# The first batch's first 512 feed-forward columns as single float32 matmuls, and the second batch's scores computed with the states in the rows

## The chip, the core and the metric

The kernel runs on one core of one Trainium2 chip. The metric is the device time of one execution in microseconds (us); three runs of the kernel before gave 684.73, 686.70 and 690.73, so the median is 686.7 us. TensorE (PE) multiplies matrices, VectorE (DVE) and ScalarE (ACT) work on elements, and SyncE (SP) issues the DMA transfers.

## The reference

The inputs are `x` (8 batches, 8 heads, 512 tokens, 64 wide), `state` (8, 8, 32 states, 64) and the weights `w_in` (512 x 2048) and `w_out` (2048 x 512). The weights come as float64 numbers, which the kernel itself turns into float32; the rest is float32.

```python
scores = scale * np.matmul(x, state.transpose(0, 1, 3, 2))     # tokens look at states
a = softmax(scores);  xread = np.matmul(a, state)
scores2 = scale * np.matmul(state, x.transpose(0, 1, 3, 2))    # states look at tokens
a2 = softmax(scores2); sread = np.matmul(a2, x)
attn = np.concatenate([xread, sread], axis=2)                  # 512 + 32 rows per batch
x = attn.transpose(0, 2, 1, 3).reshape(B * S, H * D)           # 4352 tokens of 512
h = x @ w_in;  g = h * np.clip(h + 3.0, 0.0, 6.0) / 6.0;  out = g @ w_out
```

## The kernel before, in words

**Two feed-forward products in float32r.** The feed-forward layer takes nearly all the time. TensorE computes it in float32r, a short form of float32, and makes up for the lost digits by splitting every operand into a high and a low part: `product` (L642) issues three matmuls, high x high, high x low and low x high, for each pair. The high part is a ScalarE cast and the low part a VectorE subtraction (`split`, L242). So every operand, the token weights `aT`, the projected weights `wp`, the hidden values `g` and `w_out`, costs one ScalarE and one VectorE instruction per tile before TensorE may use it.

**Steps.** The first product folds the attention read into `w_in`: `wprime` (L424) computes state x `w_in` once per batch and 512-column chunk, and `first` (L653) multiplies it with the token softmax `aT`: 2 groups of heads x 3 matmuls of 128x512 for each of 128 columns of the hidden layer (a step). ScalarE and VectorE then apply the activation into `g`, and `second` (L693) adds `g` times `w_out` to four accumulators: 4 products of 3 matmuls. There are 16 steps for a batch; the first two batches are interleaved by segments: batch 0 steps 0 to 3 (chunk 0), batch 1 steps 0 to 7, the rest of batch 0, the rest of batch 1, then the others in turn.

**Two ways to the token softmax.** `tokens_by_rows` (L507, batches 0 and 1 before) computes scores with the tokens in the rows: 2 x 8 float32 matmuls of 128x64 (L527), the softmax (`softmax_parts`, L479), then transposes on TensorE (L544) and the split. `scores_by_columns` (L551) with `tokens_by_columns` (L559, the other batches) computes 8 small matmuls of 64x32 weights and 512 columns each (L419), and VectorE transposes blocks of 32x32 before and after the softmax. The state softmax (`states`, L573) needs the second form in any case; batches 0 and 1 compute it later, at their eighth to twelfth step.

**Weights.** Each weight tile arrives as 64-bit words. ScalarE (L294, L298) and VectorE (L302, L306, L313) turn the words into float32; `w_out` is then split into halves (L335, L337). Tiles go through `raw` buffers or through `early0` to `early3`, which share space with later tiles.

**What sets the order.** The code hands every operation to `Plan` with a cost, a rank and its dependencies; `Plan.order` (L54) plays them through in a model of the four queues and writes the order in which each engine gets its instructions. Each engine then works its own list strictly in that order, so a waiting instruction holds all behind it. Until the first feed-forward matmul, the gaps that the plan foresees on TensorE are filled with transposes of the identity (L901). All loads are issued by SP, in the planned order.

Of the kernel before, what the change touches and what calls it, by code (L numbers as in the profile page):

```python
# [20 lines left out]
class Plan:  # L21
# [32 lines left out]
    def order(self):  # L54
# [93 lines left out]
def tile_state_attention_then_hardswish_ffn(  # L148
# [51 lines left out]
    w_in_sb = cpool.tile([P, NQ, DFF], F32, name="w_in_sb")  # L200
# [13 lines left out]
            "g_hi": 3, "g_lo": 3, **{f"early{k}": 1 for k in range(4)}, **BANKS,  # L214
# [34 lines left out]

    HOMES = [(c, half) for c in range(NCH - 2, NCH) for half in ("hi", "lo")]  # L250
    w_out_sb = {}

    def w_out_key(k, half):
        home = (k // FPC, half)
        return (f"early{HOMES.index(home)}", "home", k) if home in HOMES else ("w_out", k, half)
# [9 lines left out]
    def weight(kind, k, n, place, rank, load_rank):  # L265
# [44 lines left out]
        def sign():  # L310
            low, high, _, _ = words()
            d = w_in_sb[:, :, ks].bitcast(U32) if kind == "in" else low
# [11 lines left out]
        if kind == "in":  # L324
            V(wide, rank, sign, [hi, lo], [("w_in", f) for f in range(k, k + n)])
            return
        V(wide, rank, sign, [hi], [lo])
        low = lambda: words()[0].bitcast(F32)
        at_home = {h: [w_out_key(f, h) for f in range(k, k + n)] for h in ("hi", "lo")}

        gone = [
            m for slot, users in plan.users.items() for m in users
            if slot[1] != "home" and slot[0] in (at_home["hi"][0][0], at_home["lo"][0][0])
        ]
        S_((0.6, 1.05)[n - 1], rank, lambda: nc.scalar.copy(w_out_of("hi", k, n), low()),  # L335
           [lo], at_home["hi"], gone)
        V(wide, rank, lambda: nc.vector.tensor_tensor(  # L337
            w_out_of("lo", k, n), low(),
            w_out_of("hi", k, n).bitcast(F32),
            op=ALU.subtract), [lo, *at_home["hi"]], at_home["lo"])  # L340
# [6 lines left out]
    def load_state(b, rank, after=()):  # L347
# [6 lines left out]
        plan.add("Q", 0.9, rank, load, (), [key], after, 64.0)  # L354
# [69 lines left out]
    def wprime(b, c, f0, f1, rank, banks=None, after=()):  # L424
# [5 lines left out]
        def wp(half):  # L430
# [5 lines left out]
            lambda q: w_in_sb[:, q, c * CH + f0 * P : c * CH + f1 * P]),  # L436
            [("stT", b)] + [("w_in", c * FPC + f) for f in range(f0, f1)], bs, after)
        for u in range(NG):
# [5 lines left out]
    def tmp(key):  # L444

        return get(key, lambda: att.tile([P, S], F32, name="tmp", bufs=10))

    def take_in(b, rank, after=(), banks=None):
# [10 lines left out]
        for q in range(NQ):  # L459
            xT = ("tmp", ("xT", b, q))  # L460
            if b >= TURNED:
                key = ("raw", ("x", b, q // 2))
                V(0.7, rank, lambda q=q, key=key, xT=xT: nc.vector.transpose(
                    tmp(xT), made[key][:, q % 2]),
                    [(*key, q % 2, u, k) for u in range(2) for k in range(D // NS)], [xT], after)
                continue
# [10 lines left out]
            S_(0.6, rank, lambda ps=ps, xT=xT: nc.scalar.copy(tmp(xT), bank(ps)), [ps], [xT])  # L477
# [29 lines left out]
    def tokens_by_rows(b, rank, after, banks=None):  # L507
# [14 lines left out]
        def scores(k):  # L522
            out = bank(ps[k]).rearrange("p (j u q n) -> p j q u n", j=J // 2, u=NG, n=NS)
            for j in range(J // 2):
                for q in range(NQ):
                    js = slice((k * J // 2 + j) * P, (k * J // 2 + j + 1) * P)
                    nc.tensor.matmul(  # L527
                        out[:, j, q], tmp(("tmp", ("xT", b, q)))[:, js], apart[:, q],
                        start=True, stop=True,
                    )  # L530
        for k in range(2):
            scores_at[b] = T(2.0, rank(1), lambda k=k: scores(k),
                             [("apart", u) for u in range(NG)]
                             + [("tmp", ("xT", b, q)) for q in range(NQ)], [ps[k]], after(1))
        for k in range(2):
# [4 lines left out]
            def turn(back=back, bt_key=bt_key):  # L540
                for g in range(NG):
# [3 lines left out]
            T(0.47, rank(4), turn, [bt_key], [back], after(4))  # L545
            split(min(rank(4), 0.0), lambda k=k: hi_lo["hi"]()[:, :, half(k)],
                  lambda k=k: hi_lo["lo"]()[:, :, half(k)],
                  lambda back=back: bank(back).rearrange("p (g t) -> p g t", g=NG),
                  [back], [("aT", b, k, "hi"), ("aT", b, k, "lo")])

    def scores_by_columns(b, rank, after=()):  # L551

        ps = [("ps_s", ("C", b, u)) for u in range(NG)]
        T(1.2, rank, lambda: all_heads(
            b, [bank(k) for k in ps], lambda q: tmp(("tmp", ("xT", b, q)))),
          [("stT", b)] + [("tmp", ("xT", b, q)) for q in range(NQ)], ps, after)
# [41 lines left out]
    def state_read(b, rank, after):  # L598
# [17 lines left out]
        for u in range(NG):  # L616
# [22 lines left out]
            [scores_at[1]])  # L639
# [13 lines left out]
    def first(n):  # L653
        b, i, _, _ = steps[n]
        ps = ("ps_h", n)
        if b < B:
# [6 lines left out]
            reads += [("wp", (b, k), f0, u, h) for u in wide for h in ("hi", "lo")]  # L663
        else:
# [6 lines left out]
        def run():  # L671
            ah, al = (made["aT", b][h]() for h in ("hi", "lo"))
# [5 lines left out]
        first_of[n] = T(1.37 if b < B else 1.45, n, run, reads, [ps], first_after.get(n, ()))  # L678


        g = lambda: get(("g", n), lambda: gp.tile([P, S], F32, name="g"))[:, :width]
# [4 lines left out]
            g(), bank(ps)[:, :width], AF.Relu, bias=three), [ps], [("g", n)])  # L686
        V(cost, n, lambda: nc.vector.scalar_tensor_tensor(  # L687
            g(), g(), 6.0, bank(ps)[:, :width], op0=ALU.min, op1=ALU.mult), [ps], [("g", n)])
        split(n, half["hi"], half["lo"], g, [("g", n)], [("g_hi", n), ("g_lo", n)], cost)
# [3 lines left out]
    def second(n):  # L693
# [3 lines left out]
        for j in range(nt):  # L697
# [7 lines left out]
            T(0.685, n + LAG + 0.5, run,  # L705
              [("g_hi", n), ("g_lo", n), w_out_key(i, "hi"), w_out_key(i, "lo")], [acc])
# [34 lines left out]
    def w_in_split(c, rank, after):  # L741

        cs = slice(c * CH // 2, (c + 1) * CH // 2)
        wp = {h: (lambda h=h: get((f"wp_{h}", (B, c)), lambda: gp.tile(
            [P, NQ, CH // 2], F32R, name=f"wp_{h}"))) for h in ("hi", "lo")}
        S_(1.2, rank, lambda: nc.scalar.copy(wp["hi"](), w_in_sb[:, :, cs]), [],
           [("wp", (B, c), "hi")], after)
        V(1.25, rank, lambda: nc.vector.tensor_tensor(
            wp["lo"](), w_in_sb[:, :, cs], wp["hi"]().bitcast(F32), op=ALU.subtract),
# [17 lines left out]
    for seg, (b, c0, c1) in enumerate(segments):  # L767
# [109 lines left out]
    for n in range(len(steps)):  # L877
# [54 lines left out]
```

## Time and profile before

| | |
|---|---|
| median of three runs | 686.7 us |
| the profiled execution | 687.1 us, of which the span of its records is 685.3 us |
| PE busy | 668.7 us (98%) |
| DVE busy | 418.1 us (61%) |
| ACT busy | 318.4 us (46%) |
| first feed-forward matmul starts | 29.41 us |

The span is the time from the first to the last record; the execution's own time is 1.8 us more. PE counts as busy also where matmuls overlap in its pipeline, so a row's length is more than its share of the stream: the distance between the starts of two matmuls tells what one costs.

### The profile page before, as it was taken

Reading aid. Unit: us, or ns where it says so; the run is one execution under the profiler, and the core shown is the slowest. Engines: PE = TensorE matmul, PEld = TensorE weight load, DVE = VectorE, ACT = ScalarE, POOL = GpSimd, SP = SyncE. Lnnn points to the kernel's source line nnn. Section 1 sums busy time; section 2 is a strip of 40 time slices with the busy share of each in tenths; the row PEclk is TensorE's granted clock in tenths of the full one; section 3 lists DMA queues with packets and bytes.
Section 4 is the critical chain, followed back from the end, with each engine's and each line's share of the span. In section 5 each row is a group of like instructions: output and inputs, shape, how many; then the busy total and the mean of one; then the engine's idle time right before and its main releaser. Section 6 shows DMA issues by size and latency. Waiting matters only on the chain.

```text
span 685.3 us, 10084 instructions
## 1 busy us (share of the span) xinstructions
PE 668.7 (98%) x4095; PEld 517.2 (75%) x4095; DVE 418.1 (61%) x729; ACT 318.4 (46%) x533; POOL 1.0 (0%) x7
## 2 busy tenths in 40 slices
PE   7798999999999999999999999999999999999997
PEld 6676677777777777787777777777777777778996
DVE  3889888859865835844486337934584444334552
ACT  4886667554523533533354333533443344333442
POOL 0000000000000000000000000000000000000000
PEclk9999999999999999999999999999999999999999
DMA  8731144343244020511040302330010001000101
GB/s 258 271 124 62 62 134 119 122 93 89 39 123 67 1 62 0 128 36 27 1 111 16 62 1 71 58 62 0 1 62 1 1 0 63 1 0 1 63 1 31
DMA packets 94126, 41.54 MB, mean 61 GB/s; under 512 B 82432, under 2 KB 84480, under 8 KB 93952
## 3 DMA queue, kind: packets, MB, share of 16 engines
q1 hardware_dynamic: 94080, 40.90, 22.6%
q8 instruction: 32, 0.52, 0.3%
q14 instruction: 14, 0.11, 0.1%
HBM read 31.98 MB, written 8.91 MB: 60 GB/s over the span
## 4 chain that ended last, share of the span: by engine, by line
PE 93%; SPq 2%; ACT 1%; DVE 1%; DMA 1%; issue 0%
PE acc L648 56%; PE ps_h L648 28%; PE ps_s L419 6%; PE ps_s L621 1%; PE ps_s L606 1%; DMA early<-in_moe_w_out_dram 1%; SPq L374 1%; SPq L353 1%; PE ps_s L527 1%; SPq L289 0%; ACT early L294 0%; ACT early L298 0%; ACT aT_hi L244 0%; DVE g L687 0%; DVE early L306 0%
## 5 line engine op out<-in xcount | busy, mean ns | idle before, releaser
L648 PE MATMUL acc<-w_out_hi,g_hi 128*128 128x512 f32 x544 | 220.7, 406 | 0.0
L648 PE MATMUL acc<-w_out_hi,g_lo 128*128 128x512 f32 x544 | 212.9, 391 | 0.0
L648 PE MATMUL acc<-w_out_lo,g_hi 128*128 128x512 f32 x544 | 212.3, 390 | 0.0
L685 ACT ACTIVATE g<-ps_h,three 128x512 f32<-128x512 f32 (+1 forms) x144 | 95.5, 663 | 209.3 <-PE ps_h L648 206.7
L687 DVE SCALAR_TENSOR_TENSOR g<-g,ps_h 128x512 f32<-128x512 f32 (+1 forms) x144 | 94.0, 653 | 141.3 <-ACT g L685 141.0
L648 PEld LDWEIGHTS acc<-w_out_hi,g_hi 128*128 128x128 f32 x544 | 102.4, 188 | 51.5 <-ACT g L685 21.4
L245 DVE TENSOR_TENSOR g_lo<-g,g_hi 128x512 fp32r<-128x512 f32 (+1 forms) x144 | 94.4, 657 | 58.3 <-ACT g_hi L244 57.3
L244 ACT CAST g_hi<-g 128x512 fp32r<-128x512 f32 (+1 forms) x144 | 85.7, 596 | 81.0 <-DVE g L687 80.9
L648 PE MATMUL ps_h<-aT_hi,wp_hi 128*128 128x512 f32 (+1 forms) x320 | 118.9, 372 | 2.6 <-DVE g L687 1.9
L648 PEld LDWEIGHTS acc<-w_out_hi,g_lo 128*128 128x128 f32 x544 | 102.2, 188 | 22.7
L648 PE MATMUL ps_h<-aT_lo,wp_hi 128*128 128x512 f32 (+1 forms) x320 | 118.2, 369 | 0.2 <-DVE aT_lo L245 0.2
L648 PE MATMUL ps_h<-aT_hi,wp_lo 128*128 128x512 f32 (+1 forms) x320 | 118.3, 370 | 0.0
L648 PEld LDWEIGHTS acc<-w_out_lo,g_hi 128*128 128x128 f32 x544 | 102.6, 189 | 18.7
L648 PEld LDWEIGHTS ps_h<-aT_hi,wp_hi 128*128 128x128 f32 x320 | 60.4, 189 | 15.2 <-DVE g L687 2.8
L648 PEld LDWEIGHTS ps_h<-aT_lo,wp_hi 128*128 128x128 f32 x320 | 60.4, 189 | 11.0 <-DVE aT_lo L245 0.5
L648 PEld LDWEIGHTS ps_h<-aT_hi,wp_lo 128*128 128x128 f32 x320 | 60.4, 189 | 10.1
L245 DVE TENSOR_TENSOR wp_lo<-ps_s,wp_hi 128x512 fp32r<-128x512 f32 (+1 forms) x70 | 41.8, 630 | 3.2 <-ACT wp_hi L244 3.2
L244 ACT CAST wp_hi<-ps_s 128x512 fp32r<-128x512 f32 (+1 forms) x70 | 35.2, 542 | 4.7 <-PE ps_s L419 4.6
L419 PE MATMUL ps_s<-w_in_sb,stT 64*32 64x512 f32 (+1 forms) x560 | 35.1, 558 | 1.7 <-DVE w_in_sb L313 1.7
L294 ACT ACTIVATE early<-early,eighth 128x1024 uint32<-128x1024 uint32 (+1 forms) x16 | 18.1, 1129 | 2.6 <-DMA early<-in_moe_w_out_dram 2.0
L609 ACT COPY tmp<-ps_s 128x512 f32<-128x512 f32 x16 | 9.3, 587 | 21.3 <-PE ps_s L606 21.3
L493 ACT ACTIVATE tmp<-tmp 128x512 f32<-128x512 f32 x16 | 10.1, 631 | 17.1 <-DVE tmp L491 16.6
(91 smaller groups left out, 409.1 us busy)
## 6 DMA issues: line engine op xcount, KB each, us to landing
out_dram<-ot SPq DMA_DIRECT2D x8, 1024.0 KB, 5.5
early<-in_moe_w_in_dram SPq DMA_DIRECT2D x7, 1024.0 KB, 5.4
xb<-in_x_dram SPq DMA_DIRECT2D x24, 256.0 KB, 4.7
raw<-in_x_dram SPq DMA_DIRECT2D x96, 64.0 KB, 2.3
early<-in_moe_w_out_dram SPq DMA_DIRECT2D x5, 1024.0 KB, 7.4
raw<-in_moe_w_out_dram SPq DMA_DIRECT2D x4, 512.0 KB
ot<-in_x_dram SPq DMA_DIRECT2D x2, 512.0 KB, 3.7
early<-in_moe_w_in_dram SPq DMA_DIRECT2D x2, 512.0 KB
```

Of the source, the lines that this page charges most:

```text
L244: S_(cost, rank, lambda: nc.scalar.copy(hi(), src()), reads, [writes[0]])
L245: V(cost, rank, lambda: nc.vector.tensor_tensor(lo(), src(), hi().bitcast(F32), op=ALU.subtract), [*reads, writes[0]], [writes[1]])
L294: nc.scalar.activation(low, low, AF.Identity, scale=0.92 * 2.0**-29, bias=eighth)
L353: nc.sync.dma_start(raw[:, u, :], st_v[b, :, :, u, :])
L374: nc.sync.dma_start(x_tile(b)[:, :, j, :], x_v[b, j])
L419: nc.tensor.matmul(out[u][cols, :], made["stT", b][rows, cols], moving(q)[rows], start=True, stop=True,)
L493: S_(0.62, rank(2), lambda: nc.scalar.activation(bt(), bt(), AF.Exp, scale=SCALE), [], [bt_key])
L527: nc.tensor.matmul(out[:, j, q], tmp(("tmp", ("xT", b, q)))[:, js], apart[:, q], start=True, stop=True,)
L609: S_(0.6, URGENT, lambda pe=pe, t_key=t_key: nc.scalar.copy(tmp(t_key), bank(pe)), [pe], [t_key])
L648: nc.tensor.matmul(ps, l, r, start=start and k == 0, stop=stop and k == n - 1)
L685: S_(cost + 0.05, n, lambda: nc.scalar.activation(g(), bank(ps)[:, :width], AF.Relu, bias=three), [ps], [("g", n)])
L687: V(cost, n, lambda: nc.vector.scalar_tensor_tensor(g(), g(), 6.0, bank(ps)[:, :width], op0=ALU.min, op1=ALU.mult), [ps], [("g", n)])
```

## The change

Four things change. (1) `plain(b, c)` is true for batch 0, chunk 0, the first four steps. For these, `wprime` copies the projected weights once as float32 (no halves), `first` issues 2 float32 matmuls instead of 6 float32r ones, the hidden values are not split, and `second` issues one float32 matmul per product instead of three. Its right operand is the decoded `w_out` as it lies in the 64-bit words, that is, every second 32-bit word. The halves of this part of `w_out` and of batch 0's token softmax are still needed for later steps and are made later (`late_halves`, `halves_of_first`). (2) Batch 1's token softmax is computed with `scores_by_columns` and `tokens_by_columns`; the same scores are computed a second time, later, for the state softmax, as batch 0 does. (3) `w_in`, one tile before, is four tiles, and the turned `x` of batches 0 and 1 and batch 0's softmax lie in tiles not yet in use. The first `w_out` pieces are loaded one by one through `raw`. (4) In `Plan.order`, an operation on TensorE that follows another on TensorE is no longer counted as waiting for its latency.

```diff
@@ Plan.order
-                ready[h] = max(ready[h], done)
+                own = e == "T" == self.ops[h][0]
+                ready[h] = max(ready[h], t + cost if own else done)
@@ wprime
-        for u in range(NG):
+        for u in range(NG) if plain(b, c) else ():
+            wp32 = lambda: get(("wp_32", (b, c)),
+                               lambda: gp.tile([P, NG, CH], F32, name="wp_32", tag="wp_hi"))
+            S_(0.06 + 0.54 * n / CH, rank, lambda u=u: nc.scalar.copy(
+                wp32()[:, u, fs], bank(bs[u])[:, :n]), [bs[u]], [("wp", (b, c), f0, u, "hi")])
+        for u in range(NG) if not plain(b, c) else ():
@@ tokens_by_rows
+            if b == 0:
+                for g in range(NG):
+                    S_(0.35, min(rank(4), 0.0), lambda g=g, k=k, turned=turned: nc.scalar.copy(
+                        a_first(g)[:, half(k)], turned()[:, g]),
+                        [back], [("w_in2", "a", g, k)])
+                continue
@@ first
+            if plain(b, i // FPC):
+                for g in wide:
+                    nc.tensor.matmul(bank(ps), made["wp_32", (b, k)][:, g, fs],
+                                     a_first(g), start=g == 0, stop=g == NG - 1)
+                return
@@ second
+                if plain(b, i // FPC):
+                    nc.tensor.matmul(bank(acc), made["g_hi", n][:, js], plain_out[i][1](),
+                                     start=opens, stop=closes)
+                    return
@@ the main loop
+    at(6, lambda: [f(6.6 + 0.2 * k) for k, f in enumerate(late_halves)])
+    at(9, halves_of_first, 9.5)
...
-            tokens_by_rows(1, lambda k: (1.0, 1.2, 1.6, 2.0, 2.4)[k],
-                           lambda k: [wp_at[0, 0, 2]])
+            rank1 = lambda k: (1.0, 1.2, 1.6, 2.0, 2.4)[k]
+            tokens_by_columns(1, rank1, scores_by_columns(1, 1.2, [wp_at[0, 0, 2]]))
```

The order on three engines changes at the places that follow. On ScalarE, between the two exponentials of batch 0's softmax (L493, `tmp`), there stood before:

```order
L493 ACTIVATE tmp<-tmp 128x512
L298 ACTIVATE early_107<-early_107 128x1024
L477 COPY tmp<-ps_s 128x512
L294 ACTIVATE early_109<-early_109,eighth 128x512
L298 ACTIVATE early_109<-early_109 128x512
L244 CAST aT_hi<-acc_309 128x2x256
L493 ACTIVATE tmp<-tmp 128x512
```

and now (the exponential is L529, the copies of `x` are L513, the softmax goes into `w_in_304`):

```order
L529 ACTIVATE tmp<-tmp 128x512
L312 ACTIVATE raw<-raw 128x512
L312 ACTIVATE early_106<-early_106 128x1024
L585 COPY w_in_304<-acc_293 128x256 x2
L529 ACTIVATE tmp<-tmp 128x512
L513 COPY w_in_316<-ps_s 128x512 x3
L585 COPY w_in_304<-acc_341 128x256 x2
L513 COPY w_in_316<-ps_s 128x512
L308 ACTIVATE raw<-raw,eighth 128x512
```

The decoding of the second `w_out` tile (L294 before, L308 on `raw` now) stood between the two exponentials and stands behind both now.

On VectorE, between the second tile of `w_in` and the subtraction of the second half's maximum in batch 0's softmax, there stood before:

```order
L313 SCALAR_TENSOR_TENSOR w_in_sb<-early_104 128x4x128
L245 TENSOR_TENSOR wp_lo<-acc_207,wp_hi 128x128
L245 TENSOR_TENSOR wp_lo<-acc_208,wp_hi 128x128
L489 TENSOR_REDUCE m_227<-ps_s 128x16
L245 TENSOR_TENSOR wp_lo<-acc_237,wp_hi 128x128
L245 TENSOR_TENSOR wp_lo<-acc_238,wp_hi 128x128
L491 TENSOR_TENSOR tmp<-ps_s,m_227 128x512
L489 TENSOR_REDUCE m_261<-ps_s 128x16
L457 COPY stT<-ps_s 128x128
L516 COPY sread_t<-stT 64x4x32 x2
L495 TENSOR_REDUCE s_289<-tmp 128x16
```

and now:

```order
L327 SCALAR_TENSOR_TENSOR w_in_206<-early_103 128x4x128
L525 TENSOR_REDUCE m_224<-ps_s 128x16
L527 TENSOR_TENSOR tmp<-ps_s,m_224 128x512
L525 TENSOR_REDUCE m_253<-ps_s 128x16
L531 TENSOR_REDUCE s_259<-tmp 128x16
L533 TENSOR_SCALAR s_259<-s_259 128x16
L534 RECIPROCAL s_259<-s_259 128x16
L494 COPY stT<-ps_s 128x128
L535 TENSOR_TENSOR tmp<-tmp,s_259 128x512
L527 TENSOR_TENSOR tmp<-ps_s,m_253 128x512
```

The four subtractions for `wp_lo` and the second batch's two copies into `sread_t` are gone from this stretch.

On TensorE, from the first feed-forward matmul to the first one of batch 1, the new order is (L728 is `first`, L766 `second` in plain float32, L441 the small matmuls of `wprime` or of the scores, L699 `product`):

```order
L728 MATMUL ps_h<-w_in_304,wp_226 128x512 x4
L441 MATMUL ps_s<-w_in_206,stT 32x256 x8
L766 MATMUL acc_390<-raw,g 128x512
L441 MATMUL ps_s<-w_in_316,stT 32x512 x8
L728 MATMUL ps_h<-w_in_304,wp_226 128x512 x2
L441 MATMUL ps_s<-w_in_206,stT 32x512 x8
```

and where batch 1's scores stood before there was this:

```order
L648 MATMUL acc_440<-w_out_hi_372,g_hi 128x512
L648 MATMUL acc_440<-w_out_lo_375,g_hi 128x512
L648 MATMUL acc_440<-w_out_hi_372,g_lo 128x512
L527 MATMUL ps_s<-sread_t,tmp 128x2x32 x16
L648 MATMUL ps_h<-aT_hi,wp_hi 128x512
```

The sixteen matmuls of L527 and the eight transposes of L544 for batch 1 are gone, and eight small matmuls (L441 on `w_in_316`, which holds the turned `x` of batch 1) stand in their place.

## Rows read from the trace of the kernel before

**Rows 1.** The page's busy times by engine: us, share of the span, instructions.

```profile
PE 668.7 (98%) x4095; PEld 517.2 (75%) x4095; DVE 418.1 (61%) x729; ACT 318.4 (46%) x533; POOL 1.0 (0%) x7
```

**Rows 2.** Busy time by stretches: length, then each engine's busy us, granted clock, DMA.

```profile
50.00:60.00 10.00, 7.89 (x38) 5.30 (x38) 9.89 (x13) 5.24 (x7) 0.00 (x0) 0.83 0.25 76
...
200.00:400.00 200.00, 200.00 (x1208) 152.22 (x1208) 119.49 (x217) 81.78 (x140) 0.00 (x0) 1.00 0.23 49
```

**Rows 3.** TensorE in order of time: start, length, line, operands, [idle before <-releaser].

```profile
27.46 0.66 PE L544 MATMUL acc<-ident,tmp 128*128 128x128 f32 x4 [0.34 <-DVE tmp L499]
...
29.41 0.48 PE L648 MATMUL ps_h<-aT_hi,wp_hi 128*128 128x512 f32 x1
...
32.04 0.39 PE L648 MATMUL ps_h<-aT_hi,wp_lo 128*128 128x512 f32 x1
34.13 0.67 PE L419 MATMUL ps_s<-w_in_sb,stT 64*32 64x256 f32 x16 [1.71 <-DVE w_in_sb L313]
...
36.23 3.68 PE L527 MATMUL ps_s<-sread_t,tmp 128*128 128x64 f32 x32
```

**Rows 4.** ScalarE in order of time, batch 0's softmax.

```profile
20.67 0.59 ACT L477 COPY tmp<-ps_s 128x512 f32<-128x512 f32 x1
23.06 0.78 ACT L294 ACTIVATE early<-early,eighth 128x512 uint32<-128x512 uint32 x1 [1.80 <-DMA early<-in_moe_w_out_dram]
...
24.77 0.63 ACT L493 ACTIVATE tmp<-tmp 128x512 f32<-128x512 f32 x1
```

**Rows 5.** VectorE in order of time, batch 0's softmax.

```profile
13.42 0.69 DVE L306 SCALAR_TENSOR_TENSOR early<-early 128x512 uint32<-128x512 uint32 x1
...
16.55 0.48 DVE L245 TENSOR_TENSOR wp_lo<-acc,wp_hi 128x128 fp32r<-128x128 f32 x2
...
17.91 0.49 DVE L245 TENSOR_TENSOR wp_lo<-acc,wp_hi 128x128 fp32r<-128x128 f32 x2 [0.28 <-ACT wp_hi L244]
...
19.82 0.46 DVE L516 COPY sread_t<-stT 64x128 f32<-64x128 f32 x2
...
21.53 0.69 DVE L499 TENSOR_TENSOR tmp<-tmp,s 128x512 f32<-128x512 f32 x1
22.14 0.68 DVE L491 TENSOR_TENSOR tmp<-ps_s,m 128x512 f32<-128x512 f32 x1
...
26.71 0.69 DVE L499 TENSOR_TENSOR tmp<-tmp,s 128x512 f32<-128x512 f32 x1
```

**Rows 6.** TensorE in order of time, steps 2 to 4 (one stretch read twice).

```profile
41.97 1.09 PE L419 MATMUL ps_s<-w_in_sb,stT 64*32 64x512 f32 x16
42.99 0.50 PE L648 MATMUL acc<-w_out_hi,g_hi 128*128 128x512 f32 x1
...
46.55 0.60 PE L544 MATMUL ps_s<-ident,tmp 128*128 128x128 f32 x4
46.90 0.48 PE L648 MATMUL acc<-w_out_hi,g_hi 128*128 128x512 f32 x1
...
49.64 0.50 PE L648 MATMUL ps_h<-aT_hi,wp_hi 128*128 128x512 f32 x1 [0.68 <-ACT aT_hi L244]
50.37 0.50 PE L648 MATMUL ps_h<-aT_lo,wp_hi 128*128 128x512 f32 x1 [0.22 <-DVE aT_lo L245]
...
54.69 0.50 PE L648 MATMUL ps_h<-aT_hi,wp_hi 128*128 128x512 f32 x1 [1.89 <-DVE g L687]
```

**Rows 7.** The same set of small matmuls, its first eight alone.

```profile
41.97 0.66 PE L419 MATMUL ps_s<-w_in_sb,stT 64*32 64x512 f32 x8
```

**Rows 8.** The chain of waits: start, length, what.

```profile
108.35 2.72 PE acc L648 x12
```

**Rows 9.** Busy time of a stretch after the longest wait, columns as in rows 2.

```profile
55.10:58.50 3.40, 3.40 (x10) 2.63 (x9) 3.35 (x5) 1.34 (x3) 0.00 (x0) 0.51 0.29 51
```

**Rows 10.** Who waited for whom on TensorE, 0 to 110 us.

```profile
PE ps_s L621 <- DVE sr L629: 0.9, 2, 0.5
```

More of the change, by code (lines that the diff above doesn't have):

```diff
@@ L213, in tile_state_attention_then_hardswish_ffn @@
             "raw": 3, "ot": 2, "xb": 1, "st_raw": 1, "stT": 2, "tmp": 10, "sr": 1, "aT": 2, "m1": 3, "s1": 3, "nm2": 3, "r2": 3, "wp": 2, "g": 2,
-            "g_hi": 3, "g_lo": 3, **{f"early{k}": 1 for k in range(4)}, **BANKS,
+            "g_hi": 3, "g_lo": 3, **{f"early{k}": 1 for k in range(4)}, **{f"w_in{c}": 1 for c in range(NCH)},
+            "w_out_hi1": 1, **BANKS,
         },
@@ L246, in split, with w_in_of, w_in_keys @@
             lo(), src(), hi().bitcast(F32), op=ALU.subtract), [*reads, writes[0]], [writes[1]])
+    plain = lambda b, c: b == 0 and c == 0
+    plain_out, late_halves = {}, []
     HOMES = [(c, half) for c in range(NCH - 2, NCH) for half in ("hi", "lo")]
     w_out_sb = {}
+    def w_in_of(c, name="w", shape=(P, NQ, CH)):
+        return get((f"w_in{c}", name), lambda: cpool.tile(
+            list(shape), F32, name=f"w_in{c}", tag=f"w_in{c}"))
+    def w_in_keys(f0, f1):
+        return [(f"w_in{f // FPC}", "w", f) for f in range(f0, f1)]
     def w_out_key(k, half):
         home = (k // FPC, half)
+        if home == (1, "hi"):
+            return ("w_out_hi1", "home", k)
         return (f"early{HOMES.index(home)}", "home", k) if home in HOMES else ("w_out", k, half)
@@ L311, in sign @@
             low, high, _, _ = words()
-            d = w_in_sb[:, :, ks].bitcast(U32) if kind == "in" else low
+            d = w_in_of(k // FPC)[:, :, k % FPC * P : (k % FPC + n) * P].bitcast(U32) if kind == "in" else low
             nc.vector.scalar_tensor_tensor(
@@ L324, in weight @@
         if kind == "in":
-            V(wide, rank, sign, [hi, lo], [("w_in", f) for f in range(k, k + n)])
+            V(wide, rank, sign, [hi, lo], w_in_keys(k, k + n))
             return
@@ L328, in weight, with halves @@
         low = lambda: words()[0].bitcast(F32)
+        if k < FPC:
+            plain_out[k] = (key, lambda: words()[0].bitcast(F32)[:, 0, :])
         at_home = {h: [w_out_key(f, h) for f in range(k, k + n)] for h in ("hi", "lo")}
[L331 to L340, printed above, removed]
+        def halves(rank):
+            gone = [
+                m for slot, users in plan.users.items() for m in users
+                if slot[1] != "home" and slot[0] in (at_home["hi"][0][0], at_home["lo"][0][0])
+            ]
+            S_((0.6, 1.05)[n - 1], rank, lambda: nc.scalar.copy(w_out_of("hi", k, n), low()),
+               [lo], at_home["hi"], gone)
+            V(wide, rank, lambda: nc.vector.tensor_tensor(
+                w_out_of("lo", k, n), low(),
+                w_out_of("hi", k, n).bitcast(F32),
+                op=ALU.subtract), [lo, *at_home["hi"]], at_home["lo"])
+        if k < FPC:
+            late_halves.append(halves)
+        else:
+            halves(rank)
     TURNED = 2
@@ L446, in tmp, with xT_key, xT @@
         return get(key, lambda: att.tile([P, S], F32, name="tmp", bufs=10))
+    def xT_key(b, q):
+        return (("w_out_hi1", "w_in3")[b], "xT", q) if b < 2 else ("tmp", ("xT", b, q))
+    def xT(b, q):
+        if b == 0:
+            return get(xT_key(0, q), lambda: cpool.tile(
+                [P, NQ, S], F32, name="xT", tag="w_out_hi1"))[:, q]
+        return w_in_of(3, "xT")[:, q] if b == 1 else tmp(xT_key(b, q))
     def take_in(b, rank, after=(), banks=None):
@@ L527, in scores @@
                     nc.tensor.matmul(
-                        out[:, j, q], tmp(("tmp", ("xT", b, q)))[:, js], apart[:, q],
+                        out[:, j, q], xT(b, q)[:, js], apart[:, q],
                         start=True, stop=True,
@@ L533, in tokens_by_rows @@
                              [("apart", u) for u in range(NG)]
-                             + [("tmp", ("xT", b, q)) for q in range(NQ)], [ps[k]], after(1))
+                             + [xT_key(b, q) for q in range(NQ)], [ps[k]], after(1))
         for k in range(2):
@@ L663, in first @@
             reads += [("wp", (b, k), f0, u, h) for u in wide for h in ("hi", "lo")]
+            if plain(b, k):
+                reads = [("w_in2", "a", g, h) for g in wide for h in range(2)]
+                reads += [("wp", (b, k), f0, u, "hi") for u in wide]
         else:
@@ L677, in run @@
             )
-        first_of[n] = T(1.37 if b < B else 1.45, n, run, reads, [ps], first_after.get(n, ()))
-        g = lambda: get(("g", n), lambda: gp.tile([P, S], F32, name="g"))[:, :width]
+        first_of[n] = T(1.95 if plain(b, i // FPC) else 1.37 if b < B else 1.45, n, run, reads, [ps], first_after.get(n, ()))
+        in_32 = plain(b, i // FPC)
+        g_key = ("g_hi", n) if in_32 else ("g", n)
+        g = lambda: get(g_key, lambda: gp.tile(
+            [P, S], F32, name="g", tag=g_key[0], bufs=3 if in_32 else 2))[:, :width]
         half = {h: (lambda h=h: get((f"g_{h}", n), lambda: gp.tile(
@@ L685, in first @@
         S_(cost + 0.05, n, lambda: nc.scalar.activation(
-            g(), bank(ps)[:, :width], AF.Relu, bias=three), [ps], [("g", n)])
+            g(), bank(ps)[:, :width], AF.Relu, bias=three), [ps], [g_key])
         V(cost, n, lambda: nc.vector.scalar_tensor_tensor(
-            g(), g(), 6.0, bank(ps)[:, :width], op0=ALU.min, op1=ALU.mult), [ps], [("g", n)])
-        split(n, half["hi"], half["lo"], g, [("g", n)], [("g_hi", n), ("g_lo", n)], cost)
+            g(), g(), 6.0, bank(ps)[:, :width], op0=ALU.min, op1=ALU.mult), [ps], [g_key])
+        if not in_32:
+            split(n, half["hi"], half["lo"], g, [g_key], [("g_hi", n), ("g_lo", n)], cost)
     part_of = {}
@@ L704, in run @@
                 product(bank(acc), [((hi[:, js], lo[:, js]), w)], opens, closes)
-            T(0.685, n + LAG + 0.5, run,
-              [("g_hi", n), ("g_lo", n), w_out_key(i, "hi"), w_out_key(i, "lo")], [acc])
+            if plain(b, i // FPC):
+                T(0.9, n + LAG + 0.5, run, [("g_hi", n), (*plain_out[i][0], "lo")], [acc])
+            else:
+                T(0.685, n + LAG + 0.5, run,
+                  [("g_hi", n), ("g_lo", n), w_out_key(i, "hi"), w_out_key(i, "lo")], [acc])
         if not closes:
```

51 lines of the change are left out of this document (30 added, 21 removed), and 2 rows, old and new, of the table weights.

## The prediction, made before the changed kernel ran

> **What bounds the kernel now.** The page's busy times come first: TensorE is busy for 98% of the span, VectorE for 61%, ScalarE for 46% [rows 1]. The table by stretches shows where the missing 2% lie. From 200 to 400 us TensorE is busy every microsecond at the full clock, with VectorE at 60% and ScalarE at 41%; from 50 to 60 us TensorE has 7.89 of 10 us and VectorE 9.89 [rows 2]. So from about 100 us on the kernel is a full TensorE stream: a microsecond of matmuls added or removed anywhere behind the start, and a microsecond of TensorE idle there, moves the end by a microsecond. What else sets the time is when the stream starts (29.41 us [rows 3]) and how often it stops in its first 65 us. The stops are in the TensorE timeline: 1.71 us before 34.13 [rows 3], 0.68, 0.22 and 1.89 us before 49.64, 50.37 and 54.69 [rows 6], and 0.9 us in two waits of the state reads [rows 10]. The sum below is made against the profiled execution, 687.1 us; the median, 686.7, is 0.4 lower, and I take that off at the end.
>
> **Term 1, the start: 29.41 becomes about 25.5, -3.9 us.** The first feed-forward matmul needs batch 0's softmax, so I follow that chain. VectorE first: between the second `w_in` tile and the second half's subtraction (22.14) stood four small subtractions for `wp_lo`, 0.48 + 0.49 us with a wait of 0.28 between, and two copies into `sread_t`, 0.46 [rows 5]. All are gone from there, 1.71 us, so the subtraction starts near 20.4 and ends near 21.1. ScalarE then: the exponential of that half began at 24.77, though its input was ready at 22.82 (22.14 + 0.68), because ScalarE's list had the decoding of the second `w_out` tile ahead of it, and that waited 1.80 us for a transfer, until 23.06 [rows 4, 5]. The new list has this decoding behind the exponential and behind the softmax copies. The exponential is now held only by the two half-width copies of the first turn (its input, L499, moves from 21.53 to 19.8), so it begins at 21.2 to 21.8, 3.0 to 3.6 us earlier. The last multiply (26.71) and the last turn on TensorE (27.46) follow by 23.9 to 24.5. Before, the first matmul came 1.95 us after that turn's start [rows 3]; now there is no low half to wait for, and turn (0.66), copy and hand-over take about 1.4. That gives 25.3 to 25.9; I take 25.5. Bounds: 27.7, if only VectorE's 1.71 us count, and 25.0.
>
> **Term 2, matmuls: +2.1 us.** A float32r matmul of 512 columns takes 2.72/12 = 0.227 us in the stream [rows 8], a product of three 0.68. Four steps have 2 products in `first` and 4 in `second`, 24 in all, and each becomes one float32 matmul of 128x512. The trace has none of that shape. The nearest is the set of eight small float32 matmuls over 512 columns, which run side by side. They leave sixteen records, two for each. The first eight end 0.66 us after the start, all of them after 1.09 [rows 6, 7], so the second records lag the first by 0.43, and the set holds TensorE for 1.02 (41.97 to 42.99 [rows 6]). A plain matmul therefore costs between 2 x 0.43 = 0.86 and 1.02. I take 0.907, four times the float32r matmul, as the lower end is the stream alone and the upper has the set's fill in it. That is 0.227 more for each product, 24 x 0.227 = +5.4 (bounds +4.3 and +8.2). Against it, batch 1 loses two score groups of 3.68 us [rows 3], some 3.5 without the overlap at the end, and two turns of 0.35 (46.55 to 46.90 [rows 6]), and gains one more set of 1.02: -3.2. In all +2.2, rounded with the overlaps to +2.1 (bounds +1.0 to +5.0).
>
> **Term 3, stops behind the start: -4.8 us.** Read from start to start, each stop is a little longer than its idle time (32.04 + 0.23 to 34.13 is 1.86, not 1.71 [rows 3]); the stops listed make some 6.2 us. The stop at 34.13 waited for a `w_in` tile behind batch 0's halves on VectorE. Now four plain matmuls (3.6 us instead of 2.7) run ahead of it, and 5 or 6 VectorE halves are gone. The stops at 49.64 to 54.69 are VectorE at its limit [rows 2]; out of that stretch go the halves of four steps' `g`, of `w_out`, `wp` and batch 0's `aT`, some 7 us of VectorE, and in come four block transposes, 2.5 us. On TensorE plain second products stand ahead of batch 1's first. The two stops of the state reads stay (0.9), and I leave 0.5 for the rest: 1.4 remain. Bounds: -6.2 and -2.
>
> **Term 4, the clock: -1.6 us.** After the 1.89 us stop the granted clock was 0.51 of full speed from 55.10 to 58.50, the 1.2 GHz level: 10 matmul records in 3.4 us, where the full clock does 15 in that time [rows 9, 8]. Without the stop before it, I expect no such stretch. Bounds: 0 and -1.7.
>
> **At no cost:** the halves made later (four casts and four subtractions for `w_out`, two each for `aT`) lie in steps 6 to 9 on ScalarE and VectorE, beside a TensorE stream with room in both from 60 us on [rows 2]; if VectorE had no room there, each would cost 0.61 us. The single `w_out` loads on SP carry the same bytes. They stand ahead of the `w_in` tile for steps 4 and 5, and that is first used behind the second batch's exponentials, so it would have to be late by over 2 us. The end of the program is unchanged.
>
> **Sum:** -3.9 + 2.1 - 4.8 - 1.6 = -8.2, so 687.1 becomes 678.9, and against the median 678.5.
>
> **The rivals.**
>
> *VectorE becomes the bound (chance 0.20).* From batch 0's last multiply (about 24.3) to batch 1's `aT_lo`, VectorE's new list has 22 full-width instructions at 0.61 (21.53 to 22.14 [rows 5]), three double-width ones (3.1), two clamps (0.8), small ones (0.9), and some 1.2 where one needs the result of the one before: 19.4 us, to 43.7. TensorE's list to the same point has 18 plain matmuls at 0.907 and three sets (0.6 + 1.02 + 1.02), 18.9 us from 25.5, to 44.4. This is a tie: the rival decides as soon as VectorE is over 0.7 us later than I reckon, and 0.1 us more on each of 30 instructions would put 2.4 us of idle back: 681. For it speaks VectorE's 9.89 of 10 us before [rows 2].
>
> *The second operand is read at half speed (chance 0.06), the way to slower.* The 16 plain matmuls of `second` read `w_out` in every second word. No row here shows TensorE reading so. If such a pass takes twice as long, 16 x 0.907 = 14.5 us come on top, about 1 of it into idle that remains: 678.5 + 13.5 = 692. Against it: VectorE reads the same words in 0.69 us (L306, 13.42), as long as neighbouring ones (L499, 21.53) [rows 5]. By the Trainium skill, "SBUF — State Buffer", section "Door 1: The DMA port swizzle", a line of SBUF has 16 bytes and two hits on a line suffice for full speed; a step of 8 bytes has two, so by this rule the rival falls; no run shown here tests it on TensorE.
>
> *The start does not move as far (chance 0.12).* The copies of batch 1's `x` (L513, three in a row) now stand ahead of the last softmax copies on ScalarE. They need x of batch 1; if they wait for it, or for TensorE's turn, the first matmul comes near 28 and the sum is -5.7: 681.
>
> **How the numbers follow.** The forecast has the remaining 0.62; with its bounds on plain matmuls and clock it spans 675 to 682. The range 674 to 685 leaves out the strided rival and half of the far ends. About 1% (6.9 us, down to 679.8) is what a measurement of this kernel tells from no change: the forecast lies beyond it by 1.3 us, most of its own span does too, and a little of the two cases at 681; that makes 0.58 for faster, 0.36 within 1%, and 0.06 slower, from the strided rival with a high price of plain matmuls.
>
> **What would show it.** The first plain matmul (L728) at 25 to 26 us; L728 and L766 starts 0.9 us apart (1.8 for L766 alone would be the strided rival); ScalarE without a wait on `w_out` before the second exponential; under 2.5 us of TensorE idle between the first matmul and 100 us, without a stretch at half the clock. A stop of 2 us before batch 1's first L699 with VectorE as the releaser would be the first rival. I am wrong if the stream starts earlier but the stops return elsewhere, or if a plain matmul costs over 1.1 us.

## The result and the profile after

The changed kernel takes 678.03 us (median of 4 runs, 677.73 to 679.04) against 685.97 for the kernel before (median of 4, 684.73 to 690.73): ratio 0.9888, 95% interval 0.9855 to 0.9921. A second set of runs gives 678.34 against 685.81: 0.9894 (0.9874 to 0.9914). The profiled execution takes 679.04 us, its span is 677.3, 8.0 less than before.

The page's busy times: TensorE has lost 2.0 us of busy time, the span 8.0; so six of the eight are idle time that is gone.

```profile
PE 666.7 (98%) x4036; PEld 507.1 (75%) x4036; DVE 416.2 (61%) x725; ACT 318.2 (47%) x536; POOL 1.0 (0%) x7
```

By stretches, columns as in [rows 2]: from 50 to 60 us TensorE now has 10.00 of 10 us at the full clock, where it had 7.89 at 0.83. VectorE still has 9.8.

```profile
40.00:50.00 10.00, 9.86 (x40) 4.25 (x39) 9.86 (x15) 6.93 (x11) 0.00 (x0) 1.00 0.00 0
50.00:60.00 10.00, 10.00 (x54) 6.25 (x53) 9.78 (x21) 8.22 (x18) 0.00 (x0) 1.00 0.01 2
```

TensorE in order of time, columns as in [rows 3]: the first plain matmul starts at 25.45 us, where the first matmul stood at 29.41.

```profile
24.30 0.66 PE L580 MATMUL acc<-ident,tmp 128*128 128x128 f32 x4 [0.27 <-DVE tmp L535]
...
25.45 3.67 PE L728 MATMUL ps_h<-w_in,wp 128*128 128x512 f32 x8
29.05 0.66 PE L441 MATMUL ps_s<-w_in,stT 64*32 64x256 f32 x16
...
39.21 5.98 PE L766 MATMUL acc<-raw,g 128*128 128x512 f32 x12
44.61 0.82 PE L699 MATMUL ps_h<-aT_hi,wp_hi 128*128 128x512 f32 x1
45.26 0.40 PE L699 MATMUL ps_h<-aT_lo,wp_hi 128*128 128x512 f32 x1
...
45.95 0.39 PE L699 MATMUL ps_h<-aT_lo,wp_hi 128*128 128x512 f32 x1
```

ScalarE: the second exponential (L529) starts at 21.66 instead of 24.77 [rows 4], and the decoding of the second `w_out` tile (L308) comes behind it without waiting.

```profile
21.12 0.65 ACT L585 COPY w_in<-acc 128x256 f32<-128x256 f32 x2 [1.11 <-PE acc L580]
21.66 0.65 ACT L529 ACTIVATE tmp<-tmp 128x512 f32<-128x512 f32 x1
22.19 1.08 ACT L513 COPY w_in<-ps_s 128x512 f32<-128x512 f32 x2
23.53 0.59 ACT L513 COPY w_in<-ps_s 128x512 f32<-128x512 f32 x1 [0.26 <-PE ps_s L508]
25.00 0.65 ACT L585 COPY w_in<-acc 128x256 f32<-128x256 f32 x2 [0.88 <-PE acc L580]
...
26.01 0.83 ACT L308 ACTIVATE raw<-raw,eighth 128x512 uint32<-128x512 uint32 x1
```

VectorE: the second half's subtraction starts at 20.29 (22.14 before [rows 5]), its last multiply at 23.56 (26.71). The lower line matters further down: batch 1's two low halves end at 44.27.

```profile
20.29 0.68 DVE L527 TENSOR_TENSOR tmp<-ps_s,m 128x512 f32<-128x512 f32 x1
...
23.56 0.69 DVE L535 TENSOR_TENSOR tmp<-tmp,s 128x512 f32<-128x512 f32 x1
...
42.99 1.28 DVE L247 TENSOR_TENSOR aT_lo<-tmp,aT_hi 128x512 fp32r<-128x512 f32 x2
```

TensorE's waits from 25 us to the end (who waits for whom: us, times, longest): one row is left, the state reads of [rows 10].

```profile
PE ps_s L672 <- DVE sr L680: 1.0, 2, 0.5
```

### The profile page after: what moved, and what is told of

The parts are those of the page before. It is cut to its first block, busy times and chain, and to the rows that moved or that the text cites. A ratio compares the mean times of both kernels' runs of the same rounds, so it can differ in the third digit from the quotient of the medians.

```text
span 677.3 us, 9947 instructions
## 1 busy us (share of the span) xinstructions
PE 666.7 (98%) x4036; PEld 507.1 (75%) x4036; DVE 416.2 (61%) x725; ACT 318.2 (47%) x536; POOL 1.0 (0%) x7
## 4 chain that ended last, share of the span: by engine, by line
PE 95%; DVE 3%; DMA 1%; ACT 1%; issue 0%; SPq 0%
PE acc L699 55%; PE ps_h L699 28%; PE ps_s L441 6%; PE acc L766 1%; PE ps_s L672 1%; PE ps_s L657 1%; DMA st_raw<-in_state_dram 1%; PE ps_h L728 1%; DVE tmp L535 0%; DVE s L531 0%; PE acc L508 0%; DVE tmp L527 0%; DVE m L525 0%; DVE early L320 0%; PE acc L580 0%
## 5 line engine op out<-in xcount | busy, mean ns | idle before, releaser
L699 PE MATMUL acc<-w_out_hi,g_hi 128*128 128x512 f32 x528 | 213.8, 405 | 0.0
L699 PE MATMUL acc<-w_out_hi,g_lo 128*128 128x512 f32 x528 | 206.2, 391 | 0.0
L699 PE MATMUL acc<-w_out_lo,g_hi 128*128 128x512 f32 x528 | 205.9, 390 | 0.0
L699 PEld LDWEIGHTS acc<-w_out_hi,g_hi 128*128 128x128 f32 x528 | 99.1, 188 | 49.3 <-ACT g L747 21.0
L699 PE MATMUL ps_h<-aT_hi,wp_hi 128*128 128x512 f32 (+1 forms) x312 | 115.9, 372 | 0.0
L699 PEld LDWEIGHTS acc<-w_out_hi,g_lo 128*128 128x128 f32 x528 | 99.1, 188 | 21.9
L699 PE MATMUL ps_h<-aT_hi,wp_lo 128*128 128x512 f32 (+1 forms) x312 | 114.7, 368 | 0.0
L699 PE MATMUL ps_h<-aT_lo,wp_hi 128*128 128x512 f32 (+1 forms) x312 | 114.6, 367 | 0.0
L699 PEld LDWEIGHTS acc<-w_out_lo,g_hi 128*128 128x128 f32 x528 | 99.4, 188 | 18.0
L699 PEld LDWEIGHTS ps_h<-aT_hi,wp_hi 128*128 128x128 f32 x312 | 58.8, 188 | 12.1 <-issue 1.4
L699 PEld LDWEIGHTS ps_h<-aT_lo,wp_hi 128*128 128x128 f32 x312 | 58.8, 188 | 10.7 <-issue 0.5
L699 PEld LDWEIGHTS ps_h<-aT_hi,wp_lo 128*128 128x128 f32 x312 | 58.8, 188 | 9.8
L441 PE MATMUL ps_s<-w_in,stT 64*32 64x512 f32 (+1 forms) x592 | 37.3, 561 | 0.0
L441 PEld LDWEIGHTS ps_s<-w_in,stT 64*32 64x32 f32 x592 | 6.7, 104 | 14.8 <-issue 11.3
L529 ACT ACTIVATE tmp<-tmp 128x512 f32<-128x512 f32 x16 | 10.1, 631 | 14.5 <-DVE tmp L527 14.4
```

Of the source, the lines that this page charges most:

```text
L441: nc.tensor.matmul(out[u][cols, :], made["stT", b][rows, cols], moving(q)[rows], start=True, stop=True,)
L529: S_(0.62, rank(2), lambda: nc.scalar.activation(bt(), bt(), AF.Exp, scale=SCALE), [], [bt_key])
L699: nc.tensor.matmul(ps, l, r, start=start and k == 0, stop=stop and k == n - 1)
```

## The experiments

The kernel before had medians of 685.34 (23 runs, beside the first four kernels), 685.11 (23 runs, the next three) and 685.81 (10 runs, the last three); each ratio is against its own. The ratio and the interval in brackets are estimated from the single runs, so the ratio need not be the quotient of the two medians.

Where the stream starts in an execution also goes with the moment at which TensorE's clock first reaches full speed (last section). That was 10.77 and 9.96 us in the profiled pair above and 9.66 in `e2_rows`, but 4.4 to 6.1 in all other profiled executions below. So their starts are set beside those of `e0_again` (the changed kernel once more, 24.25 us) and `e5_fill` (up to 50 us the order of the kernel before, 28.30 us), not beside 25.45 and 29.41.

**Only the scores with the states in the rows, nothing plain** (`e1_no_plain`); the late halves and the full-width copies go back with it:

```diff
-    plain = lambda b, c: b == 0 and c == 0
+    plain = lambda b, c: False
```

> The change without its plain float32 part: batch 0's first four steps are split and multiplied in three matmuls as before; the second batch's scores by columns, the tiles and the order rule stay. My theory (plain matmuls buy VectorE room, and VectorE is what stops TensorE before 55 us): TensorE saves 24 x 0.2 = 5 us of plain matmuls, but VectorE gets back some 16 subtractions of 0.2 to 0.7 us, about 8 us, in a stretch where it has no room, so TensorE stops for 4 to 6 us before the second batch's first product, perhaps with a stretch at half clock: 683 to 687 us, about the kernel before. Rival (the gain is TensorE work saved by the scores by columns): the 5 us come off the changed kernel's 678: 672 to 674.

684.56 us, ratio 0.9985 (0.9964 to 1.0005), as expected. The stream starts at 25.48, then TensorE stands for 5.11 us at batch 1's softmax; the granted clock is 0.50 from 45.36 us, still inside the stop, to 52.19.

```profile
47.23 0.80 PE L699 MATMUL ps_h<-aT_hi,wp_hi 128*128 128x512 f32 x1 [5.11 <-ACT aT_hi L246]
```

The table by stretches shows who is at work in this stop: ScalarE has 4.00 and VectorE 3.90 of 4 us.

```profile
44.00:48.00 4.00, 0.77 (x1) 0.29 (x1) 3.90 (x9) 4.00 (x7) 0.00 (x0) 0.67 0.00 0
```

The expectation named VectorE alone, and the releaser is a ScalarE cast. But that cast starts as soon as VectorE's first transposed half is there (the first of the two ends near 46.5):

```profile
45.82 1.30 DVE L618 STREAM_TRANSPOSE tmp<-tmp 128x512 f32<-128x512 f32 x2
46.55 1.21 ACT L246 CAST aT_hi<-tmp 128x512 fp32r<-128x512 f32 x2
```

Without the plain steps the earlier start buys nothing that can be told from noise; the halves of four steps are then still to be made and the wait moves to the next place.

**Only the plain steps** (`e2_rows`), batch 1's scores as before:

```diff
-            tokens_by_columns(1, rank1, scores_by_columns(1, 1.2, [wp_at[0, 0, 2]]))
+            tokens_by_rows(1, rank1, lambda k: [wp_at[0, 0, 2]])
```

> The change without its part on the second batch's scores: tokens by rows as before, plain float32 kept. My theory: the start stays at 25 to 26 us, TensorE gets the 3.2 us of my second term back, VectorE is relieved of four block transposes, so the stops between 26 and 57 us stay under 1 us: 680 to 682. Rival (the scores by columns carry the gain): 685 to 687.

681.09 us, ratio 0.9926 (0.9902 to 0.9949), as expected; the stream starts at 25.52 and TensorE's stops behind it come to 0.5 us. The two parts alone give 0.8 and 4.3 us, together 7 to 8: each is covered by the other's limit.

**The order rule taken back** (`e3_rule`):

```diff
-                ready[h] = max(ready[h], t + cost if own else done)
+                ready[h] = max(ready[h], done)
```

> The changed kernel with the old rule in the planner (an operation on TensorE waits for the latency of the one before it). My theory: the rule moves a few instructions and is worth less than 1.5 us: 678 to 680. Rival (the rule's order is what removes the stops): stops of over 2 us before 60 us, 681 or more.

677.99 us, ratio 0.988 (0.9826 to 0.9934): the rule is worth nothing that can be measured.

**The second `w_out` tile decoded early again** (`e4_early`), by its rank; other decodings move a little with it:

```diff
-        (1.5, "out", 1, 1, ("raw", ("out", 1)), 1.5, -4.0), ...
+        (1.5, "out", 1, 1, ("raw", ("out", 1)), -4.0, -4.0), ...
```

> The changed kernel with the decoding of the second w_out tile put back ahead of batch 0's second exponential on ScalarE, by its rank; the planner moves a few things with it. My theory (first term): the exponential waits again for that transfer, until about 23 us, the first feed-forward matmul comes at 28.5 to 29.5 instead of 25.45, and nearly all of that reaches the end, less the 0.5 to 1 us of stops that vanish: 680.5 to 682. Rival A (VectorE's list, tied with TensorE's until 45 us, is the real bound, so the start does not matter): below 679. Rival B (the exponential is held by something else): first matmul stays below 26.5 and the time at 678.

681.89 us, ratio 0.9936 (0.9917 to 0.9955), as expected. On ScalarE the decoding waits for its transfer, ahead of the exponential, as before [rows 4]:

```profile
22.25 0.78 ACT L308 ACTIVATE raw<-raw,eighth 128x512 uint32<-128x512 uint32 x1 [1.93 <-DMA raw<-in_moe_w_out_dram]
```

and on TensorE the first plain matmul comes at 28.54:

```profile
28.54 1.95 PE L728 MATMUL ps_h<-w_in,wp 128*128 128x512 f32 x4
```

More than one instruction holds it. The exponential starts at 23.75, and the sum behind it on VectorE only at 25.44, because the rest of that tile's decoding now stands ahead of the sum there; in `e0_again` these two are 0.68 us apart, here 1.69.

```profile
23.75 0.63 ACT L529 ACTIVATE tmp<-tmp 128x512 f32<-128x512 f32 x1
25.44 0.68 DVE L531 TENSOR_REDUCE s<-tmp 128x16 f32<-128x512 f32 x1
```

So the early decoding of one tile, on both engines, undoes about half of the gain.

**The kernel before with that decoding behind the exponential** (`e6_behind`):

```diff
-        S_((0.7, 1.2)[n - 1], rank, low_digits, [key], [lo])
+        S_((0.7, 1.2)[n - 1], rank, low_digits, [key], [lo], [exp_at[0, 1]] if ... ("out", 1) else ())
```

> The kernel before, with only the decoding of the second w_out tile held until after batch 0's second exponential. My theory (first term): the exponential starts at about 22.9 instead of 24.77, right behind the subtraction, the first feed-forward matmul at 27.0 to 28.0 instead of 29.41, and the end moves by 1.4 to 2.5 us: ratio 0.9965 to 0.998. Rival (another wait takes its place, the x of the second batch or VectorE): first matmul after 28.8, ratio 0.999 to 1.001.

684.38 us, ratio 0.998 (0.9966 to 0.9994). The stream starts at 27.54, as expected, but between the medians the end moves by 0.7 us and not by 1.4 to 2.5:

```profile
21.62 0.68 DVE L491 TENSOR_TENSOR tmp<-ps_s,m 128x512 f32<-128x512 f32 x1
22.75 0.59 ACT L244 CAST aT_hi<-acc 128x512 fp32r<-128x512 f32 x1 [1.16 <-PE acc L544]
23.23 0.63 ACT L493 ACTIVATE tmp<-tmp 128x512 f32<-128x512 f32 x1
27.54 0.48 PE L648 MATMUL ps_h<-aT_hi,wp_hi 128*128 128x512 f32 x1
```

Beside `e5_fill`, whose order is the old one here, the start is only 0.8 us earlier. There the same decoding waited 0.30 us for its transfer, where it waited 1.80 in [rows 4]; what it costs depends on when the transfer lands in an execution:

```profile
21.95 0.77 ACT L294 ACTIVATE early<-early,eighth 128x512 uint32<-128x512 uint32 x1 [0.30 <-DMA early<-in_moe_w_out_dram]
28.30 0.48 PE L649 MATMUL ps_h<-aT_hi,wp_hi 128*128 128x512 f32 x1
```

What holds the softmax next is VectorE's list, with the subtraction at 21.62 (20.29 in the changed kernel), and then the cast of the first half on ScalarE, which waits for TensorE until 22.75.

**The kernel before with its long stop filled** (`e5_fill`): the matmuls of batch 0's later scores are issued three times, with the same result, where TensorE stood 1.89 us [rows 6].

```diff
-        T(1.2, rank, lambda: all_heads(
-            b, [bank(k) for k in ps], lambda q: tmp(("tmp", ("xT", b, q)))),
+        T(1.2, rank, lambda: [all_heads(
+            b, [bank(k) for k in ps], lambda q: tmp(("tmp", ("xT", b, q))))
+            for _ in range(3 if b == 0 else 1)],
```

> The kernel before, with batch 0's late scores (the set of sixteen matmul records at 51.72 us) issued three times instead of once into the same place, so that TensorE has about 2 us more work inside the stop of 1.89 us before 54.69 and the result is the same. My theory (fourth term: TensorE's stop is what the clock fell after): the stop nearly vanishes, no stretch at half clock follows at 55 us, and the time falls by 1.2 to 1.7 us: ratio 0.9975 to 0.9985. Rival (the clock falls there for another reason): the granted clock is again about 0.5 for some 3.4 us, ratio 1.000 or a little more.

686.45 us, ratio 1.0027 (1.0007 to 1.0048): slower, against the expectation. Three of its twelve runs took 689.9 to 690.6 us; the other nine have a median of 686.2, still 1.1 above. The trace has what was wanted, 48 records for 16, a stop of 0.19 us, and 50 to 60 us at the full clock. TensorE in order of time:

```profile
50.63 2.81 PE L419 MATMUL ps_s<-tmp,stT 64*32 64x512 f32 x48
53.62 0.50 PE L649 MATMUL ps_h<-aT_hi,wp_hi 128*128 128x512 f32 x1 [0.19 <-DVE g L688]
```

and, by stretches,

```profile
50.00:60.00 10.00, 9.81 (x79) 6.00 (x78) 9.77 (x12) 5.14 (x8) 0.00 (x0) 1.00 0.31 107
```

Matmul for matmul, it is 1.1 us ahead of the kernel before when the stream starts, 2.4 at 62 us, and 1.4 from 160 us on. So at the filled place this execution gains the 1.3 us that were expected. About 0.9 is lost again at a new stop on `g`, which the kernel before does not have (TensorE's waits from 60 us on):

```profile
PE ps_h L649 <- DVE g L688: 0.7, 1, 0.7
```

Nor was this execution free of half clock: its clock records have 0.5 from 8.01 to 11.42 us, before the stream starts. Why the median rose is open.

**The plain second product on adjacent words** (`e7_contig`); the output of these steps is another, since `w_in` stands in for `w_out`:

```diff
-    nc.tensor.matmul(bank(acc), made["g_hi", n][:, js], plain_out[i][1](),
+    nc.tensor.matmul(bank(acc), made["g_hi", n][:, js], w_in_of(0)[:, i, :],
```

> The changed kernel, where the plain matmuls of the second product read neighbouring words (columns of w_in in place of the decoded w_out), so the first four steps' part of batch 0's output is not the reference's. In the changed kernel a half of such a matmul takes 0.451 us from start to start, where a half of the first product, whose operand has neighbouring words, takes 0.429. My theory (the step of 8 bytes costs these 5%): 0.429 here. Rival (something else in the second product costs them): 0.451 again.

678.49 us in one run, span 675.8. The two records of each matmul follow one another at 0.429 us, as expected, against 0.450 in the changed kernel, there on `raw` and `early` tiles alike: reading every second word costs 5%. The twelve records that take 5.98 us at 39.21 in the changed kernel take 5.31 here; 0.3 of the difference is a short stop inside that set (more below). Little of this reaches the end: TensorE is 1.1 us ahead of `e0_again` at 53 us, meets a wait for VectorE that the changed kernel does not have, and the span is 0.3 shorter.

```profile
37.83 5.31 PE L766 MATMUL acc<-w_in,g 128*128 128x512 f32 x12
...
56.46 1.09 PE L657 MATMUL ps_s<-ident,tmp 128*128 128x128 f32 x8 [0.58 <-DVE wp_lo L247]
```

**How close VectorE is.** In the last set, the changed kernel ran again and beside it with the subtractions for the low halves of batch 1's softmax issued twice (`e8_vec2`) and four times (`e9_vec4`):

```diff
-        V(cost, rank, lambda: nc.vector.tensor_tensor(
-            lo(), src(), hi().bitcast(F32), op=ALU.subtract), [*reads, writes[0]], [writes[1]])
+        V(cost, rank, lambda: [nc.vector.tensor_tensor(
+            lo(), src(), hi().bitcast(F32), op=ALU.subtract) for _ in range(times)],
+            [*reads, writes[0]], [writes[1]])
...
+                  [("aT", b, g, "hi"), ("aT", b, g, "lo")], times=2 if b == 1 else 1)
```

> The changed kernel once more, as the base of the two runs beside it. Expected: 677.7 to 678.6 us, TensorE's first plain matmul at 25.3 to 25.6 us, no stretch at half clock behind it.

678.34 us, first plain matmul at 24.25, a microsecond earlier than expected (more below).

> The changed kernel, with each of the two subtractions for the low halves of batch 1's softmax issued twice: 2 x 0.61 = 1.2 us more on VectorE, same results, same order on every engine. Theory: after the change VectorE is ahead of TensorE at this place. The low halves end at about 43.64 and 44.27 us, TensorE reaches the matmuls that read them at 45.26 and 45.95, so 1.6 us are covered. Then no new stop over 0.3 us and a time within 0.5 us of the changed kernel. Rival (the tie reckoned before the run, VectorE decides from 0.7 us on): a stop of 0.5 us or more on the low halves or on g, and 0.5 to 1.2 us more.

680.35 us, 2.0 more than `e0_again`; in the profiled pair of spans, 677.4 to 676.1, 1.3 more. The theory fell. There is no stop at the softmax, as it said, but the whole list of VectorE behind it is late, and TensorE stands at the next chunk's `wp_lo`, 12 us further on. The set of small matmuls ahead of it, too, holds TensorE for 1.02 us until the next matmul, where it holds it 0.59 in `e0_again`; the table of waits does not list that. First the table, then the set here and in `e0_again`:

```profile
PE ps_s L673 <- DVE sr L681: 1.0, 2, 0.5
PE ps_s L658 <- DVE wp_lo L247: 0.6, 1, 0.6
```

```profile
53.45 1.09 PE L442 MATMUL ps_s<-w_in,stT 64*32 64x256 f32 x16
54.47 0.50 PE L700 MATMUL ps_h<-aT_hi,wp_hi 128*128 128x512 f32 x1
```

```profile
53.33 0.66 PE L441 MATMUL ps_s<-w_in,stT 64*32 64x256 f32 x16
```

> The same, with each subtraction issued four times: 6 x 0.61 = 3.7 us more on VectorE. Theory: the second low half comes at 47.9 instead of 44.3, TensorE wants it at 45.95, so about 2.0 us of stop in all, on the low halves or on g behind them: 679.7 to 680.5 us. If a stop of this length brings TensorE's half clock, as the records show it behind the 1.89 us stop of the kernel before, a stretch of about 3.4 us at half clock follows and 1.7 us come on top: 681 to 682.5. Rival (VectorE tight over the whole stretch): 3 to 3.7 us more without half clock. If VectorE has more room than I read, less than 1 us more.

682.85 us, 4.5 more for 3.7 us of VectorE; spans 680.4 to 676.1. That is above every range that was set, and nearest to the rival. Both places stop now:

```profile
PE ps_h L700 <- DVE aT_lo L247: 2.3, 2, 1.8
PE ps_s L673 <- DVE sr L681: 1.0, 2, 0.5
PE ps_s L658 <- DVE wp_lo L247: 0.6, 1, 0.6
```

So a microsecond more on VectorE at 43 us is a microsecond or more of time: the cover of 1.6 us that I read at one place ended at another. And 0.48 and 1.81 us of idle (42 to 48 us) were not followed by half clock in this execution: 1.00 from 40 to 60 us.

## Why the prediction was right

**Term 1, the start (-3.9): held, -3.96** in the profiled pair. Its steps came within a few tenths: subtraction 20.29 (forecast 20.4), exponential 21.66 (21.2 to 21.8), first matmul 25.45 (25.5). The experiments show why neither half of the edit does it: with ScalarE's order alone (`e6_behind`) the start is 27.54, with the early decoding put back into ScalarE's and VectorE's lists (`e4_early`) 28.54, and only with both 24.25 to 25.5 (single executions, which can lie a microsecond apart by their first matmuls' pace, see the end). The two lists hold the same softmax in turn. The 1.80 us wait that the term started from belongs to one execution, though; in `e5_fill` it was 0.30.

**Term 2, matmuls (+2.1): held, some tenths too high.** The records of L728 follow at 0.429 us, so a matmul takes 0.86; those of L766 at 0.450, 0.90. That is 8 x 0.18 + 16 x 0.22 = +5.0 over a product of three at 0.68, where 5.4 was reckoned. The strided rival asked for 1.8 and fell. By the Trainium skill, "SBUF — State Buffer", section "Door 1: The DMA port swizzle", two hits on a 16-byte line give full bandwidth, so such a step should cost nothing. The trace does not quite agree: 0.450 in the changed kernel against 0.429 in `e7_contig` is 5%, and the measurement decides.

**Term 3, stops (-4.8): held.** 1.4 us were to remain; the waits show 1.0, and between the eighth and ninth record of the set at 39.21 the distance is 0.76 instead of 0.45, a short stop that the table of waits does not list. But the rival that VectorE becomes the bound was nearer than its 0.20: `e8_vec2` loses all that is added, and in `e7_contig` a TensorE that is faster waits. The tie that I reckoned for the softmax is real, but it is narrowest further on, at the next chunk's `wp` and `wp_lo`, which my reckoning did not have.

**Term 4, the clock (-1.6): right for the profiled execution, too large for the median.** Before, one stretch at half clock, 55.14 to 58.55 us; after, none behind the start. But the mean clock of the other executions of the kernel before falls in two groups: 28 of 56 runs have 0.998 or more and a median of 685.10, 25 have 0.994 to 0.996 and 686.14 (the other three took 690.7 to 693.6). The second group is itself split, 9 runs up to 685.23 and 16 from 686.07 on. So the profiled execution, 0.996 and 687.1 us, had the stretch, and at least half of the runs probably did not; a mean does not tell where it fell, and `e5_fill`, which took the stretch away, did not get faster in its median. It need not fall here: `e5_fill` had one from 8.01 to 11.42 us, `e6_behind` one from 8.54 to 11.95 and one from 49.50 to 52.91. The two groups' medians lie 1.0 us apart, so I take the term to be worth 1.0 us at most against the median; no run shows this by itself.

**The sum.** -8.2 on 687.1 was the forecast for the profiled execution, and -8.06 came (687.1 to 679.04). At the matmul of 126 us it is 8.66 ahead; 0.5 comes back between 340 and 500 us, in three steps at the sets of small matmuls for later batches' scores. Such a set, at 350.24 us, held TensorE 1.01 us before; now, one product earlier in the order, at 340.90, it holds it 1.21. Why is open. Between medians the gain is less, 7.1 to 7.9 us. The step that failed is the base: 686.7 was the median of three runs, and three sets of 10 to 23 gave 685.1 to 685.8. A base about a microsecond too high and a sum up to a microsecond too large left 678.5 against 678.03. That the two errors nearly cancel is luck; the mechanism, term by term, is what held. The span of 675 to 682 does not follow from the two bounds named for it either: those of plain matmuls and clock give 677.3 to 683.0.

**The start does not move as far: fell.** The three copies of `x` (L513) stand ahead of the last softmax copies, but end at 24.12, before these start (25.00), which wait for TensorE's turn.

## What to carry to other kernels

A softmax that passes between two engines is held by both lists; shorten both, and look at each instruction ahead of it for a transfer that it waits for. Where two engines tie, look for cover at every later hand-over of the loaded engine, not at the first one: work added at one place stopped TensorE 12 us behind it. And set a profiled execution against many runs before you take its clock for the kernel's.

## What the runs showed that I had not expected

The first plain matmul starts at 25.45 us in one execution and at 24.25 in another of the same kernel. It goes with the pace of TensorE's first matmuls: the same eight transposes, in the changed kernel's two profiles (TensorE in order of time),

```profile
7.30 1.92 PE L508 MATMUL acc<-ident,xb 128*128 128x128 f32 x8
```

and in `e0_again`

```profile
6.42 1.04 PE L508 MATMUL acc<-ident,xb 128*128 128x128 f32 x8
...
24.25 3.67 PE L728 MATMUL ps_h<-w_in,wp 128*128 128x512 f32 x8
```

take 1.92 and 1.04 us. They also start 0.9 us apart, but that does not decide it: in `e2_rows` they start at 6.54 and take 1.92, and the stream starts at 25.52; in `e8_vec2` they start at 6.90 and take 1.04, and it starts at 24.37. The clock records of the first two reach full speed at 9.96 and 4.79 us. In the profiled execution of the kernel before it was 10.77, so the pair that gave -3.96 is alike in this; a pair that is not would have shown a microsecond more or less.

Nor does the length of a stop decide the half clock here. It came behind 1.89 us in the kernel before, inside the 5.11 of `e1_no_plain`, and in `e6_behind` behind stops of 0.50, 0.68 and 0.22 within 3 us; behind 0.48 and 1.81, three microseconds apart, it did not come in `e9_vec4`. What decides it is open.
